# Three of the seven weight combinations of the last stage are split into two halves when they are made, and stored and loaded as halves

## The chip, the cores and the metric

The kernel runs on one core of one Trainium2 chip. The metric is the device time of one execution in microseconds. The engines are TensorE (PE), VectorE (DVE), ScalarE (ACT), GpSimd (POOL) and SyncE (SP), which here issues the DMA transfers. Line numbers are those of the kernel before.

## The reference

```python
A = sm(q, k_lm); Bm = sm(q_lm, k_lm); C = sm(q_lm, k)      # softmax of scaled products, 32 landmarks
Z = ...                                                    # start of the iteration
for _ in range(6):
    Z = 2 * Z - Z @ Bm @ Z
x = A @ Z @ C @ v                                          # 4 x 8 heads, 576 tokens, head size 64
x = x.reshape(2304, 512)
h = x @ w_in                                               # first FFN, d_ff 2048
x = np.maximum(0.01 * h, h) @ w_out
xn = x / np.sqrt(np.mean(x * x, axis=-1, keepdims=True) + 1e-06) * rms_g
g = xn @ w_gate                                            # second FFN, d_ff 1536
out = (g / (1 + np.exp(-g)) * (xn @ w_val)) @ w_out2
```

All inputs and the output are fp32.

## The kernel before

**Precision.** Large products run as three passes on fp32r halves: an operand x is split into hi (x cast to fp32r) and lo (x minus hi, in fp32r), and a product is the sum of three terms of halves. So each operand of a large product costs a cast on ACT or DVE and a subtraction on DVE or POOL (`split_steps`, L1330) before PE can use it.

**Stages.** Until some 391 us the landmark attention runs beside the first FFN: `chain` (L598) makes the scores and the iteration with many small fp32 matmuls (b<-qt,kt, b<-kt,qsum, b<-rz, b<-ident,e), and between these stand the units of the first FFN, six matmuls b<-at,mm (L1140) and twelve py<-gs,w (L1211) each. From there to 657 us the first half of the second FFN runs (`gv`, L1619): the products with w_gate and w_val as 36 groups, each of which is a block of tokens b and a block f of columns. The order of the groups is (f, b) = (0,0), (1,0), (0,1), (1,1), (0,2), (1,2) and so on. From 657 us `out_pair` (L1875) runs nine pairs of the product with w_out2.

**Seven products.** Both halves of the second FFN use seven products in place of eight, on combinations of the operands' quarters: for the right-hand operand these are B11, B21, B22, T1, T2, T3 and T4. A group does them in this order, each six matmuls in three passes: A11 B11, S2 T2, S3 T3, S1 T1, A12 B21, A22 T4, S4 B22. `gv_rest` (L1661) adds them up on DVE: `gs<-hs,b` when the second is there, `gs<-gs,py` twice (for the third and the fourth), `ct<-gs,py` (c21, for the sixth) and `ct<-gs,py` (c12, for the last), with the products `us<-hs,ct` and `us<-ct,gs` behind them. Each addition also gives a bank of PSUM back to PE.

**Operands of gv.** `prep_x(b)` (L1529) makes the combinations of x of one block of tokens: the subtractions for T1, T3, T2 and T4 go to POOL or DVE, in the tiles called `misc`, and each is split into tiles called at, mm or w. The first group that needs block b is number 2b. `prep_w` does the same for the gate and value weights, from the `raw` tiles that w_gate, w_val, w_out2 are loaded to.

**Operands of the last stage.** `prep_o(p)` (L1717) makes, for six pairs of blocks of w_out2 rows, the seven combinations in the two `raw` tiles of the pair, and stores each (128 KB) in DRAM (`store_o`, L1735, 42 stores, 155 to 250 us). `load_o(k)` (L1749) loads each combination for the last stage, 768 KB, when its place is free, from 624 to 661 us; then `split_o` (L1762) splits it in two halves with a cast and a subtraction of 768 columns each. `prep_u` (L1819) prepares the left-hand operand u from DRAM.

**Order.** No order is written out. A planner (class `Order`, L93) takes steps (`yield`) of many tasks, each with a due time, costs and its possible engines (`pool_dve` is POOL or DVE, `act(n) + dve2(n)` ACT or DVE), and always places the step that is best by its own table of costs. Each engine runs its instructions in the placed order, SP its DMA issues too. So a change of a few steps can move every later instruction.

Of the kernel before, what the change touches and what calls it, by code (L numbers as in the profile page):

```python
# [9 lines left out]
F32 = mybir.dt.float32  # L10
F32R = mybir.dt.float32r
# [8 lines left out]
P = 128  # L20
# [207 lines left out]
def pe(n, count=1, more=0):  # L228
    return [("pe", int(count * (n * 0.4258 + 10.3)) + more)]
# [10 lines left out]
def act(n):  # L240
    return [("act", n + 50)]
# [6 lines left out]
def dvep(n):  # L248
    return [("dvep", int(n * 1.04) + 67)]


def dve2(n):
    return [("dvep", int(n * 0.52) + 68)]


def pool(n):
    return [("pool", int(n * 2.1) + 150)]


def pool_dve(n):  # L260
    return pool(n) + dvep(n)


def sp(nbytes):
    return [("sp", int(nbytes / 360))]


def pause(ns=0):
    return [(None, ns)]


def landing(ns, now):
    return [(None, ns + 2500 * (now > 30000))]
# [3 lines left out]
def landmark_attention_then_two_ffns(  # L277
# [13 lines left out]
    nc = tc.nc  # L291
# [22 lines left out]
    dram = ctx.enter_context(tc.tile_pool(name="dram", bufs=1, space=DRAM))  # L314
# [9 lines left out]
    order = Order(PAR["window"], PAR["slope"], PAR["bias"], rings)  # L324
# [24 lines left out]

    HM = DM // 2  # L350
    NP2 = NF2 // 2
    wo_dram = [dram.tile([P, NP2, HM], F32, name=f"wo_dram{k}") for k in range(7)]
    u_dram = dram.tile([P, NF2, NT], F32, name="u_dram")

# [55 lines left out]
    def after(made):  # L410
# [9 lines left out]
    nc = SimpleNamespace(  # L420
        scalar=nc.scalar, vector=order.vector, gpsimd=Seen(nc.gpsimd, after), tensor=nc.tensor,
        sync=nc.sync,
    )
    engine = {"act": nc.scalar, "dve": nc.vector, "pool": nc.gpsimd}

    def copy(e, out, src):
        if e == "act":
            nc.scalar.copy(out, src)  # L428
        else:
            engine[e].tensor_copy(out, src)  # L430
# [828 lines left out]
    B11, B21, B22, T1, T2, T3, T4 = range(7)  # L1259
# [70 lines left out]
    def split_steps(parts):  # L1330

        for hi, lo, src, n in parts:
            e = yield act(n) + dve2(n), []
            copy(e, hi, src)
            e = yield pool(n) + dvep(n), []
            engine[e].tensor_sub(lo, src, hi.bitcast(F32))
# [380 lines left out]
    def prep_o(p):  # L1717

        yield pause(0), [f"out2 {2 * p}", f"out2 {2 * p + 1}"]
        (ra, ta), (rb, tb) = o_raw[2 * p], o_raw[2 * p + 1]  # L1720
        a, b = (t.bitcast(F32).rearrange("p (k n) -> p k n", n=HM) for t in (ta, tb))
        src = {B11: a[:, 0], T1: a[:, 2], T2: a[:, 3],
               B21: b[:, 0], B22: b[:, 1], T3: b[:, 2], T4: b[:, 3]}
        sums = {T1: (a[:, 1], a[:, 0]), T3: (b[:, 1], a[:, 1]),
                T2: (b[:, 1], a[:, 2]), T4: (b[:, 0], a[:, 3])}
        for k in (B11, B21, B22):
            order.aside(store_o(p, k, src[k]))
        for k in (T1, T3, T2, T4):
            e = yield pool_dve(HM), []
            engine[e].tensor_sub(src[k], *sums[k])  # L1730
            order.aside(store_o(p, k, src[k]))
        yield pause(0), [f"o{p},{k}" for k in range(7)]
        order.free(ra, rb)

    def store_o(p, k, t):  # L1735
        yield sp(P * 1024), []
        nc.sync.dma_start(wo_dram[k][:, p], t)
        yield pause(2500), []
        order.done(f"o{p},{k}")

    ND = NP2 * P
    o_home = {}
# [5 lines left out]

    def load_o(k):  # L1749
        at, off, event = o_place[k]  # L1750
        yield sp(P * 4 * NP2 * HM), [event] + [f"o{p},{k}" for p in range(NP2)]
        v = home[at][:, off:off + OW].rearrange("p (t a n) -> p t a n", t=2, n=HM)
        o_home[k] = v
        hi, lo = v[:, 0], v[:, 1]
        nc.sync.dma_start(lo.bitcast(F32), wo_dram[k])
        yield landing(3000, order.now), []
        order.done(f"o_in{k}")
        order.add(
            due_o(0) + o_order.index(k) * PAR["pair"] // 7, PAR["split_o"], split_o(k, hi, lo)
        )  # L1760

    def split_o(k, hi, lo):  # L1762
        yield pause(0), [f"o_in{k}"]
        h = NP2 // 2
        yield from split_steps([
            (hi[:, x:x + h], lo[:, x:x + h], lo[:, x:x + h].bitcast(F32), h * HM) for x in (0, h)
        ])
        order.done(f"wo{k}", early=600)
# [106 lines left out]
    def out_pair(n):  # L1875
        pp, t = {}, {}

        def step(name, l, r, tag=None, needs=()):
            yield pe(HM, 3 * NP2), list(needs) + ([(tag, 1)] if tag else []) + [
                f"U{n},{l}", f"wo{r}"  # L1880
            ]
            if tag:
                pp[name] = bank(tag)
            hi, lo = u_hl[n, l]
            m = 0
            for x, i in ((hi, 0), (hi, 1), (lo, 0)):
                for p in range(NP2):
                    nc.tensor.matmul(  # L1888
                        pp[name][:, :HM], x[:, p, :], o_home[r][:, i, p, :],
                        start=(tag is not None and m == 0), stop=(m == 3 * NP2 - 1),  # L1890
                        skip_group_check=True,
                    )
                    m += 1
            order.free(hi)
# [70 lines left out]
    with tc.manual_schedule():  # L1965
# [28 lines left out]
        def due_o(n):  # L1994

            return due2(len(seq)) + PAR["pair"] * n
# [27 lines left out]
        for p in range(NP2):  # L2024
            order.add(due(PAR["o_from"] + PAR["o_step"] * (2 * p + 2)), 0, prep_o(p))


        for b in range(B):
            when = first(lambda j, f: j == 2 * b)
            for g in range(NG):  # L2030
                before = PAR["chain"][b] + PAR["load"] - g * 200 + PAR["form"]
# [23 lines left out]
        def start_second():  # L2055
            yield pause(0), [f"a{NB - 1},{g}" for g in range(NG)] + [
                f"chain{B - 1},{g}" for g in range(NG)
            ]
            att.release()
            open_p2a()  # L2060
            nc.sync.dma_start(g_sb, rms_g)
            nc.scalar.mul(g_sb, g_sb, 0.375 * DM ** 0.5 * 2.0 ** -24)
            order.done("p2a")
            for j in range(NB):
                order.add(due2(j // 2), PAR["norm"], norm(j))
            for b in range(NGR):
                for h in range(2):
                    order.add(due2(place[0, b]), PAR["prep"], load_x(b, h))
                order.add(due2(place[0, b]), PAR["prep"], prep_x(b))
            for f in range(NF2):  # L2070
                order.add(due2(place[f, 0]), PAR["prep"], prep_w(f))
            order.add(due2(0), 0, gv(0))
            for i, k in enumerate(o_order):
                order.add(due_o(0) + i * PAR["pair"] // 7, PAR["load_o"], load_o(k))
            for n in range(NG2):
                order.add(due_o(n), PAR["load_u"][min(n, 2)], load_u(n))
                order.add(due_o(n), PAR["prep_u"], prep_u(n))
            order.add(due_o(0), 0, out_pair(0))
# [66 lines left out]
```

## Time and profile before

| | us |
|---|---|
| median of 3 runs (796.16 to 796.9) | 796.31 |
| the profiled execution | 798.18 |
| its span, first to last instruction | 796.4 |
| PE busy | 786.6 |
| DVE busy | 597.0 |
| ACT busy | 345.0 |
| POOL busy | 145.1 |

The granted clock of TensorE is 1.00 of full speed throughout. A timeline row gives the start, the recorded duration, the engine and line, the operation and its tiles (out<-in, the names of the program), the shape, how many of the same stand in the row, and in brackets how long the engine had been idle ahead of it and for what. Operations that DVE runs back to back overlap in the records, so that the distance from start to start is shorter than the duration.

### The profile page before, as it was taken

Reading aid. Unit: us, or ns where it says so; the run is one execution under the profiler, and the core shown is the slowest. Engines: PE = TensorE matmul, PEld = TensorE weight load, DVE = VectorE, ACT = ScalarE, POOL = GpSimd, SP = SyncE. Lnnn points to the kernel's source line nnn. Section 1 sums busy time; section 2 is a strip of 40 time slices with the busy share of each in tenths; the row PEclk is TensorE's granted clock in tenths of the full one; section 3 lists DMA queues with packets and bytes.
Section 4 is the critical chain, followed back from the end, with each engine's and each line's share of the span. In section 5 each row is a group of like instructions: output and inputs, shape, how many; then the busy total and the mean of one; then the engine's idle time right before and its main releaser. Section 6 shows DMA issues by size and latency. Waiting matters only on the chain. (4 is left out here: it accounts for less than half of the span.)

```text
span 796.4 us, 16707 instructions
## 1 busy us (share of the span) xinstructions
PE 786.6 (99%) x6508; PEld 748.7 (94%) x6508; DVE 597.0 (75%) x1202; ACT 345.0 (43%) x777; POOL 145.1 (18%) x183
## 2 busy tenths in 40 slices
PE   8999999999999999999999999999999999999998
PEld 7687996999999879999999999999999999999998
DVE  5997867844556776579998777676666699999981
ACT  4885365433434548655752332223232164332220
POOL 2535100000013332111222421122221000000000
PEclk9999999999999999999999999999999999999999
DMA  9985645565446134455411432322331595555501
GB/s 326 356 303 144 206 151 148 170 196 187 159 138 211 58 117 157 156 175 147 129 42 59 166 113 93 109 69 90 112 112 56 165 332 170 146 146 158 161 27 54
DMA packets 84320, 119.72 MB, mean 150 GB/s; under 512 B 7824, under 2 KB 62608, under 8 KB 84240
## 3 DMA queue, kind: packets, MB, share of 16 engines
q1 hardware_dynamic: 84240, 118.64, 45.4%
q8 instruction: 51, 0.84, 0.4%
q14 instruction: 29, 0.24, 0.1%
HBM read 81.86 MB, written 36.77 MB: 149 GB/s over the span
## 5 line engine op out<-in xcount | busy, mean ns | idle before, releaser
L1211 PE MATMUL py<-gs,w 128*128 128x288 f32 x1536 | 223.2, 296 | 1.2 <-issue 0.9
L1211 PEld LDWEIGHTS py<-gs,w 128*128 128x128 f32 x1536 | 208.8, 188 | 10.0 <-issue 7.3
L1140 PE MATMUL b<-at,mm 128*128 128x288 f32 x768 | 120.3, 297 | 0.8 <-DVE mm L74 0.7
L1140 PEld LDWEIGHTS b<-at,mm 128*128 128x128 f32 x768 | 106.9, 188 | 7.1 <-issue 4.0
L1158 ACT ACTIVATE gs<-b 128x288 fp32r<-128x288 f32 x128 | 52.5, 410 | 112.9 <-PE b L1140 94.4
L74 DVE TENSOR_TENSOR gs<-hs,gs 128x288 fp32r<-128x288 f32 x95 | 45.8, 486 | 52.0 <-ACT hs L1161 44.1
L74 DVE TENSOR_TENSOR ct<-gs,py 128x384 f32<-128x384 f32 x72 | 39.5, 549 | 27.8 <-PE py L1613 27.8
L74 POOL TENSOR_TENSOR gs<-hs,gs 128x288 fp32r<-128x288 f32 x33 | 27.0, 817 | 156.4 <-ACT hs L1161 120.3
L1683 ACT ACTIVATE hs<-b 128x384 f32<-128x384 f32 x36 | 17.7, 492 | 86.6 <-PE b L1613 86.6
L74 DVE TENSOR_TENSOR gs<-gs,py 128x384 f32<-128x384 f32 x72 | 39.7, 552 | 16.7 <-PE py L1613 14.4
L1161 ACT ACTIVATE hs<-b 128x288 f32<-128x288 f32 x128 | 52.3, 408 | 0.0
L1712 ACT ACTIVATE ct<-ct 128x384 f32<-128x384 f32 x36 | 18.9, 526 | 69.4 <-DVE ct L74 69.4
L1613 PE MATMUL b<-w,wt 128*128 128x384 f32 x180 | 35.4, 337 | 0.0
L1613 PE MATMUL b<-w,mm 128*128 128x384 f32 x180 | 35.4, 337 | 0.0
L1613 PE MATMUL py<-w,wt 128*128 128x384 f32 x180 | 34.6, 338 | 0.1
L1613 PE MATMUL py<-w,mm 128*128 128x384 f32 x180 | 34.6, 336 | 0.0
L474 ACT ACTIVATE raw<-raw 128x512 f32<-128x512 f32 x52 | 33.8, 677 | 0.0
L1613 PEld LDWEIGHTS py<-w,mm 128*128 128x128 f32 x180 | 31.6, 188 | 0.4 <-DVE gs L74 0.3
L1613 PEld LDWEIGHTS py<-w,wt 128*128 128x128 f32 x180 | 31.7, 188 | 0.3 <-DVE gs L74 0.3
L1613 PEld LDWEIGHTS b<-w,wt 128*128 128x128 f32 x180 | 31.9, 188 | 0.0
L1613 PEld LDWEIGHTS b<-w,mm 128*128 128x128 f32 x180 | 31.8, 188 | 0.0
L74 DVE TENSOR_TENSOR gs<-hs,b 128x384 f32<-128x384 f32 (+1 forms) x45 | 23.5, 523 | 9.5 <-PE b L1613 4.9
(309 smaller groups left out, 1534.4 us busy)
## 6 DMA issues: line engine op xcount, KB each, us to landing
u_dram<-us SPq DMA_DIRECT2D x36, 384.0 KB, 2.3
raw<-w_out SPq DMA_DIRECT2D x20, 512.0 KB, 4.4
y_dram<-ys SPq DMA_DIRECT2D x56, 144.0 KB, 1.9
yin<-u_dram SPq DMA_DIRECT2D x20, 384.0 KB, 5.1
raw<-w_gate SPq DMA_DIRECT2D x12, 512.0 KB, 4.1
raw<-w_val SPq DMA_DIRECT2D x12, 512.0 KB, 5.0
wo_dram<-raw SPq DMA_DIRECT2D x42, 128.0 KB, 1.8
qt<-qT SPq DMA_DIRECT2D x8, 576.0 KB, 6.7
```

The costliest lines, as they stand in the source:

```text
L74: self.last = make(*args, **kwargs)
L474: nc.scalar.activation(high.bitcast(F32), high.bitcast(F32), AF.Prelu, scale=2.0 ** -112, alpha=2.0 ** 32)
L1140: nc.tensor.matmul(ph[:, :SB], w[b, c][:, g, o:o + P], x[j][:, g, :], start=(n == 0), stop=(n == 3 * NG - 1),)
L1158: nc.scalar.activation(g_hi[u], ph[:, :SB], AF.Prelu, alpha=0.01)
L1161: nc.scalar.activation(hs, ph[:, :SB], AF.Prelu, alpha=0.01)
L1211: nc.tensor.matmul(yacc[i][d][:, :SB], w[f][:, d * P:(d + 1) * P], x[u], start=(f == f0 and n == 0), stop=(f == f1 - 1 and n == 2),)
L1613: nc.tensor.matmul(pp[:, :GB], w[f][:, i, c * P:(c + 1) * P], x[b][k][:, c, :], start=(first and n == 0), stop=(n == 5), skip_group_check= ...
L1683: nc.scalar.activation(sg, pp["a"][:, :GB], AF.Silu)
L1712: nc.scalar.activation(t["c12"], t["c12"], AF.Silu)
```

## The change

For T4, B22 and B21 (`apart`) the split is done when the combination is made: `apart_o` casts it into a quarter of the `raw` tiles that is spare by then (or becomes spare when B11 or T1 of the pair is stored), subtracts in place, and stores both halves, 128 KB each, in `wo_parts`. `load_o` loads both halves at once, 1536 KB, straight to their places, and there is no `split_o` for these three. The other four combinations stay as they were.

```diff
+    wo_parts = [dram.tile([P, 2, NP2, HM], F32, name=f"wo_parts{k}") for k in range(7)]
...
+        spare_at = {T4: (a[:, 1], []), B22: (a[:, 0], [f"o{p},{B11}"]),
+                    B21: (a[:, 2], [f"o{p},{T1}"])}
         for k in (B11, B21, B22):
-            order.aside(store_o(p, k, src[k]))
+            if k not in apart:
+                order.aside(store_o(p, k, src[k]))
...
+        for k in apart:
+            order.aside(apart_o(p, k, src[k], *spare_at[k]))
...
+    apart = (T4, B22, B21)
+
+    def apart_o(p, k, t, hi, before):
+        yield pause(0), before
+        hi = hi.bitcast(F32R)
+        yield from split_steps([(hi, t.bitcast(F32R), t, HM)])
+        for i, part in enumerate((hi.bitcast(F32), t)):
+            yield sp(P * 1024), []
+            nc.sync.dma_start(wo_parts[k][:, i, p], part)
+        yield pause(2500), []
+        order.done(f"o{p},{k}")
...
+        if k in apart:
+            nc.sync.dma_start(v.bitcast(F32), wo_parts[k])
+            yield landing(3000, order.now), []
+            order.done(f"wo{k}")
+            return
         nc.sync.dma_start(lo.bitcast(F32), wo_dram[k])
```

Since the planner places everything anew, instructions move on every engine from some 155 us on. Three places follow; w_1582 and w_1589 are the same tile, as are w_113 and w_120, and lines of the new program are one to 26 higher.

DVE, from the last additions of group (0,1)'s successor (1,1) to the first of group (0,2), before; the cast mm<-misc and the subtraction mm<-misc,mm of 128x768 under it are T2 of block 2, whose sum POOL has made:

```order
L74 TENSOR_TENSOR mm<-misc,mm 128x768
L74 TENSOR_TENSOR gs_5339<-gs_5339,py 128x384 x2
L74 CAST mm<-misc 128x768
L74 TENSOR_TENSOR misc<-yin,misc 128x768
L74 TENSOR_TENSOR ct<-gs_5339,py 128x384
L74 TENSOR_TENSOR mm<-misc,mm 128x768
L74 TENSOR_TENSOR us<-hs,ct 128x384
L74 TENSOR_TENSOR ct<-gs_5339,py 128x384
L74 TENSOR_TENSOR at<-misc,at 128x768
L74 TENSOR_TENSOR us<-ct,gs_5339 128x384
L74 TENSOR_TENSOR gs_5339<-hs,b_5639 128x384
```

And now:

```order
L74 TENSOR_TENSOR ct<-gs_5385,py 128x384
L74 TENSOR_TENSOR mm<-misc,mm 128x768
L74 TENSOR_TENSOR us<-hs,ct 128x384
L74 TENSOR_TENSOR ct<-gs_5385,py 128x384
L74 TENSOR_TENSOR misc<-q,misc 128x2x96
L74 TENSOR_TENSOR misc<-ys,misc 128x2x288
L74 TENSOR_TENSOR us<-ct,gs_5385 128x384
L74 CAST mm<-misc 128x768
L74 TENSOR_TENSOR misc<-yin,misc 128x768
L74 TENSOR_TENSOR mm<-misc,mm 128x768
L74 TENSOR_TENSOR at<-misc,at 128x768
L74 TENSOR_TENSOR gs_5385<-hs,b_5696 128x384
```

The two rows that make the sum of T2 (misc<-q,misc and misc<-ys,misc) came from POOL to DVE, and the whole of T2 went from ahead of both ct additions to behind them.

PE in the last chain, at some 259 to 270 us, before; L948 and L631 are the small fp32 groups, L1140 and L1211 the first FFN:

```order
L1211 MATMUL py<-gs,w_1582 128x288 x12
L948 MATMUL b_3632<-qt,kt 32x288 x4
L948 MATMUL b_3633<-qt,kt 32x288 x4
L631 MATMUL b_3648<-kt,qsum_3587 32x304 x4
L631 MATMUL b_3653<-kt,qsum_3627 32x304 x4
L1140 MATMUL b_3666<-at,mm 128x288 x6
L631 MATMUL b_3676<-kt,qsum_3587 32x304 x4
L631 MATMUL b_3681<-kt,qsum_3627 32x304 x4
L1211 MATMUL py<-gs,w_113 128x288 x12
```

And now:

```order
L1212 MATMUL py<-gs,w_1589 128x288 x12
L949 MATMUL b_3660<-qt,kt 32x288 x4
L949 MATMUL b_3661<-qt,kt 32x288 x4
L1141 MATMUL b_3674<-at,mm 128x288 x6
L632 MATMUL b_3690<-kt,qsum_3614 32x304 x4
L632 MATMUL b_3695<-kt,qsum_3654 32x304 x4
L1212 MATMUL py<-gs,w_120 128x288 x12
L632 MATMUL b_3732<-kt,qsum_3614 32x304 x4
L632 MATMUL b_3737<-kt,qsum_3654 32x304 x4
L1141 MATMUL b_3752<-at,mm 128x288 x6
```

Where two fp32 groups stood with one first-FFN group between them, there are three with two between them; a little further on, another such group stands apart.

SP, the loads ahead of the last stage, before (w, wt and mm take B21, T4 and B22; the u loads are those of the second block):

```order
L1755 DMA w_1582<-wo_dram_80 128x1536
L1700 DMA u_dram<-us 128x768
L1810 DMA w_1582<-u_dram 128x6x128 x2
L1810 DMA at<-u_dram 128x6x128 x2
L1755 DMA wt<-wo_dram_85 128x1536
L1755 DMA mm<-wo_dram_81 128x1536
L1700 DMA u_dram<-us 128x768 x2
L1810 DMA yin<-u_dram 128x6x128 x4
```

And now:

```order
L1777 DMA w_1589<-wo_parts_80 128x3072
L1701 DMA u_dram<-us 128x768
L1777 DMA wt<-wo_parts_85 128x3072
L1777 DMA mm<-wo_parts_81 128x3072
L1701 DMA u_dram<-us 128x768
L1836 DMA w_1589<-u_dram 128x6x128 x2
L1836 DMA at<-u_dram 128x6x128 x2
L1701 DMA u_dram<-us 128x768
L1836 DMA yin<-u_dram 128x6x128 x4
```

The four u loads stood ahead of T4 and B22 and stand now behind both, which are twice as long, and behind a store.

## Rows read from the trace of the kernel before

**Rows 1.** The page's busy times (share, instructions), and PE's waits: us, times, longest.
```profile
PE 786.6 (99%) x6508; PEld 748.7 (94%) x6508; DVE 597.0 (75%) x1202; ACT 345.0 (43%) x777; POOL 145.1 (18%) x183
...
PE b L1888 <- ACT q L428: 0.6, 1, 0.6
PE b L1443 <- DVE ct L74: 0.4, 1, 0.4
```

**Rows 2.** Windows: stretch, length, busy us of each engine, clock, DMA share, GB/s.
```profile
160.00:225.00 65.00, 65.00 (x516) 62.43 (x515) 32.90 (x74) 25.35 (x64) 4.60 (x6) 1.00 0.56 181
...
440.00:660.00 220.00, 220.00 (x1266) 220.00 (x1265) 158.94 (x294) 69.17 (x134) 45.69 (x54) 1.00 0.39 132
660.00:675.00 15.00, 14.85 (x126) 14.65 (x124) 15.00 (x22) 6.69 (x11) 0.00 (x0) 1.00 0.55 163
```

**Rows 3.** Timeline of DVE from the first group of block 1 to block 2.
```profile
397.82 1.76 DVE L74 TENSOR_TENSOR w<-misc,w 128x768 fp32r<-128x768 f32 x1
...
409.52 0.55 DVE L74 TENSOR_TENSOR gs<-hs,b 128x384 f32<-128x384 f32 x1 [0.50 <-PE b L1613]
410.59 0.55 DVE L74 TENSOR_TENSOR gs<-gs,py 128x384 f32<-128x384 f32 x1 [0.51 <-PE py L1613]
...
413.26 0.35 DVE L74 TENSOR_TENSOR at<-q,at 128x192 fp32r<-128x192 f32 x1
...
414.20 0.55 DVE L74 TENSOR_TENSOR ct<-gs,py 128x384 f32<-128x384 f32 x1
...
418.44 1.21 DVE L74 TENSOR_TENSOR gs<-gs,py 128x384 f32<-128x384 f32 x2
420.70 1.08 DVE L74 CAST mm<-misc 128x768 fp32r<-128x768 f32 x1 [1.05 <-POOL misc L74]
...
423.03 0.94 DVE L74 TENSOR_TENSOR mm<-misc,mm 128x768 fp32r<-128x768 f32 x1
423.90 0.55 DVE L74 TENSOR_TENSOR us<-hs,ct 128x384 f32<-128x384 f32 x1
424.37 0.54 DVE L74 TENSOR_TENSOR ct<-gs,py 128x384 f32<-128x384 f32 x1
```

**Rows 4.** Timeline of DVE, a cast of the same size in the first FFN.
```profile
371.74 0.56 DVE L74 CAST w<-misc 128x768 fp32r<-128x768 f32 x1
```

**Rows 5.** Timeline of POOL beside the cast at 420.70.
```profile
420.61 0.75 POOL L74 TENSOR_TENSOR misc<-misc 128x256 f32<-128x256 f32 x1
```

**Rows 6.** Timeline of PE, products of the third, fourth and fifth group.
```profile
409.33 1.22 PE L1613 MATMUL py<-w,wt 128*128 128x384 f32 x6
...
421.92 1.20 PE L1613 MATMUL b<-w,wt 128*128 128x384 f32 x6
422.96 0.86 PE L1613 MATMUL b<-mm,wt 128*128 128x384 f32 x4
424.03 0.62 PE L1613 MATMUL b<-mm,wt 128*128 128x384 f32 x2 [0.22 <-DVE mm L74]
```

**Rows 7.** Timeline of PE in the last chain: a plain group, one between fp32 groups.
```profile
248.71 0.95 PE L1140 MATMUL b<-at,mm 128*128 128x288 f32 x6
...
262.08 1.06 PE L1140 MATMUL b<-at,mm 128*128 128x288 f32 x6
```

**Rows 8.** Timeline of PE and DVE at the start of the last stage.
```profile
672.58 2.27 PE L1888 MATMUL b<-q,mm 128*128 128x256 f32 x18
673.20 0.41 DVE L74 TENSOR_TENSOR us<-gs,py 128x256 f32<-128x256 f32 x1
...
675.45 2.41 PE L1888 MATMUL b<-q 128*128 128x256 f32 x18 [0.60 <-ACT q L428]
```

**Rows 9.** DMA issues on SP (timeline), and windows as in rows 2.
```profile
645.44 1.45 SPq L1810 DMA_DIRECT2D w<-u_dram  x2
...
644.00:658.00 14.00, 14.00 (x83) 14.00 (x82) 13.53 (x22) 10.11 (x16) 1.84 (x1) 1.00 1.00 316
658.00:668.00 10.00, 10.00 (x86) 10.00 (x86) 10.00 (x15) 4.51 (x8) 0.00 (x0) 1.00 0.40 132
```

More of the change, by code (lines that the diff above doesn't have):

```diff
@@ L1730, in prep_o @@
             engine[e].tensor_sub(src[k], *sums[k])
-            order.aside(store_o(p, k, src[k]))
+            if k not in apart:
+                order.aside(store_o(p, k, src[k]))
+        for k in apart:
+            order.aside(apart_o(p, k, src[k], *spare_at[k]))
         yield pause(0), [f"o{p},{k}" for k in range(7)]
         order.free(ra, rb)
+    apart = (T4, B22, B21)
[8 more added lines that the diff above has]
+        order.done(f"o{p},{k}")
     def store_o(p, k, t):
@@ L1750, in load_o @@
         at, off, event = o_place[k]
-        yield sp(P * 4 * NP2 * HM), [event] + [f"o{p},{k}" for p in range(NP2)]
+        yield sp(P * 4 * NP2 * HM * (1 + (k in apart))), [event] + [
+            f"o{p},{k}" for p in range(NP2)
+        ]
         v = home[at][:, off:off + OW].rearrange("p (t a n) -> p t a n", t=2, n=HM)
```

## The prediction

> **What bounds the kernel now.** I looked first at the waits of TensorE, because PE is busy 786.6 us of the span [rows 1]: a kernel like this gains or loses only where PE stops or does more. Its waits come to a few microseconds, and two of them lie at places that the change touches, 0.6 us for a cast at the start of the last stage and 0.4 us for a DVE result in a norm [rows 1]. Then the windows: in the stretch where the weights of the last stage are made, PE is busy 65.00 of 65 us and DVE 32.90; from 440 to 660 us PE has no gap at all; at the start of the last stage DVE is busy 15.00 of 15 us and PE loses only 0.15 [rows 2]. Last come the timelines of DVE, POOL and PE around one hand-over of the second FFN [rows 3 to 6], found from the order of the changed program: it is the one place where the new order puts a long chain of one engine straight in front of PE.
>
> All durations are of the profiled execution, 798.18 us with a span of 796.4; the median of the runs is 796.31. A change in the span is added to the median, since the 1.8 us around the span stay. A measurement of this kernel can tell some 0.2% (1.6 us) from no change.
>
> **Part 1: splitting early, and storing halves.** 18 casts and 18 subtractions of 128x256 are added at some 155 to 285 us, spread over ACT, DVE and POOL, and 18 more stores of 128 KB. PE is full in that stretch and DVE half idle [rows 2], and nothing there feeds PE within microseconds, so I take nothing for them; without that cover 18 pairs would cost some 18 x 0.6 us (a third of the 0.87 us of a 128x768 pass each [rows 3]), 11 us. What they do cost is order: the planner re-places everything behind them. In the last attention chain the small fp32 groups (qt,kt and kt,qsum) no longer stand in a row, so PE changes between fp32 and fp32r twice more, in and out. An h group of six between two such groups is recorded with 1.06 us, a plain one with 0.95 [rows 7]. Four changes at 0.11 us are +0.4 us; bounds 0 and 0.9.
>
> **Part 2: the hand-over to the third token block, where the time goes.** Before, POOL made T2 of this block (misc<-q,misc and misc<-ys,misc), and DVE only cast it: the cast began at 420.70, having waited 1.05 us for POOL, and PE reached its second product at 422.96 and the third pass of it at 424.03, 0.22 us late [rows 3, 6]. In the new order POOL has other work, and DVE makes T2 itself, *behind* the c12 addition (ct<-gs,py) of the group before. That addition needs the last product of that group, which ends when the next group starts, at 421.92. So a chain on one engine now lies between the end of one group and the second product of the next:
> PE's end is seen by DVE some 0.19 us later (409.33 against 409.52 [rows 3, 6]): 422.11. c12 takes 0.47 us (like the one from 423.90), the two pieces of T2 0.94 (like the two from 413.26 to 414.20), us<-ct,gs 0.47, all start to start: 423.99 [rows 3]. The cast of 128x768 is 0.56 recorded where DVE has SBUF to itself, which is 0.48 start to start [rows 4]; beside a POOL operation it was 1.08 [rows 3, 5]. With 0.48 the high half is there at 424.47, and PE has stood since 422.96: 1.5 us. Two of the three passes of the product take 2/3 of 1.04 us and end at 425.2. The low half needs the T4 subtraction (0.87) and its own 0.87, with 0.08 to its recorded end: 426.3. The third pass starts there instead of at 424.03: +2.25 us if DVE comes to c12 on time.
>
> Does it? Ahead of c12, DVE now has three more passes of 128x768 (3 x 0.87), two more casts (2 x 0.48), the two pieces of T3 (0.94) and one copy less (0.5): +4.0 us. Its cover: before, DVE was through with the same list at 419.65 (418.44 and 1.21), the two operations still to come before c12 take 0.93, so there are 1.5 us to 422.11, and two idle gaps of 0.50 and 0.51 [rows 3]. That leaves it 1.5 us late. Against it, DVE passes that ran beside POOL took 1.76 us and not 0.95 (397.82 [rows 3]); with the POOL work gone one such pass returns 0.8 us. I take 0.8 us late. Together +3.0 us; bounds 2.2 (on time) and 4.3 (1.5 late, the cast at 1.08). PE is busy without gaps behind this place [rows 2], so nothing gives it back.
>
> On this sum a rule bears that the trace does not carry. The sum above takes start to start; DVE's record from 423.90 has 0.55 us and the next starts at 424.37, inside it [rows 3]. The Trainium skill (VectorE: DVE Perf Modes, The DRAIN you can't avoid) says that the next operation does not start before the pipe of the one ahead is empty. If that meant the recorded end, each of the eight links would be 0.08 us longer and the term 3.6 us; the rows speak for start to start.
>
> **Part 3: the start of the last stage.** Six subtractions of 0.87 us leave DVE and six casts leave ACT; two casts come to DVE instead. The PE wait there is 0.60 us at 675.45, for the cast q<-misc of S2 of the second token block [rows 1, 8]. That chain begins with us<-gs,py, which needs the end of the product ahead of 672.58 and ran only at 673.20, behind a 0.87 us pass. With DVE free it can run at 672.7, and the chain moves 0.5 us forward, leaving 0.1. So the 5.2 us of DVE work are worth -0.5 us (bounds -0.6 and 0): the other subtractions were already hidden. The tail of the kernel is untouched.
> The loads of the three combinations are doubled to 1536 KB. The u loads of the second block, issued from 645.44 before, now stand behind T4, B22 and a store, so at some 654.5 to 657 us. DMA is full to 658 (316 GB/s) and drops to 132 GB/s in the ten microseconds behind it [rows 9]. What is left to move after 658 is then those 1.32 MB and 2.36 MB more, 3.68 MB, which take 11.6 us at 316 GB/s: all is landed by 669.6, the four u loads ahead of the last store and load, at some 665 to 668. DVE wants the first at about 670 to 672. It fits, by 2 to 5 us: nothing.
>
> **Part 4, small.** The 0.4 us wait of the norm [rows 1] is for a DVE operation beside which POOL ran; the new order moves POOL's work, so -0.2, the middle between losing the wait and keeping it.
>
> Sum: +0.4 + 3.0 - 0.5 - 0.2 = +2.7 us: a span of 799.1, a profiled execution of 800.9, and 796.31 + 2.7 = 799.0 us.
>
> **Rivals.**
> A, not slower: the T2 chain is hidden. DVE runs c12 and T2 well before PE asks, as it did with POOL's help (PE waited 0.22 us). For it: DVE has idle time before this place and loses POOL's interference. Against it: c12 cannot begin before 421.92 whatever DVE does, since it reads the last product, and program order on DVE is fixed. It decides if PE's second product came more than 2.2 us later than 422.96 for another reason. Then -0.5 - 0.2 + 0.4 = -0.3: 796.0.
> B, the waits go and the new order costs nothing anywhere: -0.6 - 0.4 = -1.0: 795.3, still within what can't be told from no change.
> C, DMA: the doubled T4 and B22 loads push the u loads past the point where DVE wants them; each microsecond later than 671 is a microsecond of PE. For it: the loads stand ahead of them in the queue, and the stretch is full. Against it: the slack above. If the 3.68 MB go at the mean of the two windows, 224 GB/s, they take 16.4 us and the last lands at 674.4: +3 on top of the sum, about 802.
> D, DVE is the bound through the first five groups: neither its idle gaps nor POOL's absence cover anything. It is then late by 4.0 - 1.5 = 2.5 us: 0.4 + 2.25 + 2.5 - 0.7 = +4.5, about 800.8.
>
> **How the numbers follow.** Forecast 0.62 (799.0, own range 797.7 to 800.4), A 0.16, B 0.06, C 0.08, D 0.08. The range holds A down to 796.0 and reaches to 801.0 on the other side, leaving out most of B and C and half of D: 0.18. Slower by over 0.2% (797.9 and above): most of the forecast, C and D, 0.74. Within: A, B and the low end of the forecast, 0.22. Faster (below 794.7): only if B is larger than any wait that I can see, 0.04.
>
> **What would show it.** In the trace of after: a wait of PE at the second product of the fifth group (b<-mm,wt), 1.2 to 2.5 us on the DVE cast and about 1 us on the subtraction, and none of over 0.3 us there proves part 2 wrong. The wait at the cast q<-misc in the last stage falls to 0.1 to 0.2 us; if it stays, part 3 is wrong. Two more changes of form in the last chain, without waits. The u loads of the second block land before 670; a PE or DVE wait on a DMA behind 667 us speaks for C. Long waits of PE on c22 at 398 to 420 us speak for D. A time below 796 says that the order mattered less than I think.

## The result and the profile after

The changed kernel takes 801.84 us (median of 4 runs, 800.72 to 802.53) against 796.27 us; the ratio taken run against run is 1.0059, with a 95% interval of 1.0045 to 1.0073. That is +4.7 us (3.6 to 5.8), where +2.7 was forecast; the two medians alone lie 5.6 us apart, within that interval. The profiled execution, 800.72 us with a span of 798.9, is the shortest of the four.

PE's waits in the trace after (us in total, times, longest), the three that answer to [rows 1] and to the 0.22 us in [rows 6]:

```profile
PE b L1614 <- DVE mm L74: 2.6, 2, 2.4
...
PE py L1614 <- DVE gs L74: 0.6, 1, 0.6
...
PE b L1914 <- ACT q L429: 0.2, 1, 0.2
```

The largest wait is new and stands at the second product of the fifth group. The timeline of PE there, of after (answers to [rows 6]):

```profile
403.68 2.38 PE L1614 MATMUL py<-w,mm 128*128 128x384 f32 x12 [0.55 <-DVE gs L74]
...
420.59 1.21 PE L1614 MATMUL b<-w,wt 128*128 128x384 f32 x6
424.22 1.55 PE L1614 MATMUL b<-mm,wt 128*128 128x384 f32 x4 [2.43 <-DVE mm L74]
425.96 1.01 PE L1614 MATMUL b<-mm,wt 128*128 128x384 f32 x2 [0.19 <-DVE mm L74]
426.76 2.73 PE L1614 MATMUL py<-mm,wt 128*128 128x384 f32 x12
```

And DVE's, answering to [rows 3]; the last row but one is the cast that PE waits for:

```profile
420.41 0.95 DVE L74 TENSOR_TENSOR mm<-misc,mm 128x768 fp32r<-128x768 f32 x1
421.28 0.55 DVE L74 TENSOR_TENSOR us<-hs,ct 128x384 f32<-128x384 f32 x1
421.75 0.55 DVE L74 TENSOR_TENSOR ct<-gs,py 128x384 f32<-128x384 f32 x1
422.21 0.35 DVE L74 TENSOR_TENSOR misc<-q,misc 128x192 f32<-128x192 f32 x1
422.48 0.75 DVE L74 TENSOR_TENSOR misc<-ys,misc 128x576 f32<-128x576 f32 x1
...
423.62 0.55 DVE L74 CAST mm<-misc 128x768 fp32r<-128x768 f32 x1
...
424.95 0.95 DVE L74 TENSOR_TENSOR mm<-misc,mm 128x768 fp32r<-128x768 f32 x1
```

Group four ends and group five begins on PE at 420.59. c12 (ct<-gs,py) could start 0.2 us later, at 420.8, and starts at 421.75: DVE is 1.0 us late. From there row follows row without idle time to the cast's end at 424.17 (423.62 and 0.55), and PE goes on at 424.22. What was not in the forecast is in the durations of the matmuls behind the wait: 1.55 us for four and 2.73 for twelve, where [rows 6] has 0.86 for four and the other rows of twelve 2.28. The windows of after show why (columns as in rows 2; the third number from the end is the granted clock):

```profile
420.00:424.00 4.00, 1.79 (x11) 1.47 (x9) 4.00 (x9) 1.00 (x2) 0.00 (x0) 1.00 0.02 4
424.00:426.00 2.00, 1.59 (x5) 1.08 (x5) 1.97 (x4) 0.83 (x1) 0.00 (x0) 0.59 0.51 197
426.00:428.00 2.00, 2.00 (x7) 2.00 (x8) 1.45 (x2) 0.00 (x0) 0.00 (x0) 0.56 0.00 0
428.00:430.00 2.00, 2.00 (x13) 2.00 (x12) 1.52 (x3) 0.00 (x0) 0.00 (x0) 1.00 0.02 4
```

After the wait PE gets 0.59 and 0.56 of full speed, so it runs at the lower of its two levels, 1.2 GHz, for most of these 4 us. The Trainium skill (TensorE: Matmul & The Clock Gate, Part 1) says that the throttled state is the default, and that activity releases it. The trace agrees as far as it goes: the clock fell behind 2.43 us in which PE stood. In the kernel before, no wait behind PE's first matmul is longer than 0.95 us, and the clock stays at 1.00 behind it; the 1.4 us for which L1044 waits there lie ahead of PE's first matmul and say nothing on this.

The last group of matmuls starts 2.35 us later in after (793.31 against 790.96). Where these lie, from the starts of the same product in before and after:

| place | before | after | difference | step |
|---|---|---|---|---|
| first FFN, ahead of the change | 135.40 | 134.25 | -1.15 | not the change: both orders are the same up to here |
| first FFN, behind the last chain | 294.64 | 293.46 | -1.18 | -0.03, early work and changes of form |
| second FFN, first product | 390.95 | 389.23 | -1.72 | -0.54, the norm's wait is gone |
| fifth group, first product | 421.92 | 420.59 | -1.33 | +0.39, c22 late in group two |
| fifth group, third pass of T2 | 424.03 | 425.96 | +1.93 | +3.26, the T2 chain |
| fifth group, product with T4 | 427.65 | 430.39 | +2.74 | +0.81, lower clock |
| last stage, S2 of block 2 | 675.45 | 677.80 | +2.35 | -0.39, last stage |

The steps behind the first row make +3.5 us. The -1.15 us in the first row come mostly from PE's first 25 matmuls, 6.31 us in before and 4.98 in after: at first one takes some 0.24 us from start to start, later 0.13, and the time of the turn differs from trace to trace (the 25 take 4.97 us in warm, 5.47 in ap_T4). The clock column reads 1.00 there all the same, so "throughout", said of the clock of before, is not shown for the first 7 us.

The other three runs of the changed kernel are 1.0 to 1.8 us longer than the profiled one, at a mean granted clock of 0.995 to 0.996 against 0.998. On a span of 800 us that is an estimated 1.6 to 2.4 us more of lacking full-speed time, so these runs lost more to the lower clock; no trace shows where.

The start of the last stage, of after (answers to [rows 8]), and DMA windows of the same stretch as in [rows 9]:

```profile
675.53 0.42 DVE L74 TENSOR_TENSOR us<-gs,py 128x256 f32<-128x256 f32 x1
...
677.80 2.42 PE L1914 MATMUL b<-q 128*128 128x256 f32 x18 [0.20 <-ACT q L429]
```

```profile
644.00:658.00 14.00, 14.00 (x82) 14.00 (x81) 13.20 (x22) 7.83 (x13) 1.84 (x1) 1.00 0.92 341
658.00:668.00 10.00, 10.00 (x80) 10.00 (x79) 10.00 (x16) 3.51 (x6) 0.00 (x0) 1.00 1.05 340
```

us<-gs,py now runs 0.2 us behind the end of its product (675.33) and the chain behind it costs 0.20 and not 0.60 us. DMA is full to 668 us, 340 GB/s where [rows 9] has 132, and neither PE nor DVE waits for it. The four u loads (w and at) land from 666.9 to 670.9 us, by the trace's landings.

### The profile page after: what moved, and what is told of

Same layout as the page of the kernel before. It is cut to its first block, busy times and chain, and to the rows that moved or that the text cites. A ratio compares the mean times of both kernels' runs of the same rounds, so it can differ in the third digit from the quotient of the medians.

```text
span 798.9 us, 16762 instructions
## 1 busy us (share of the span) xinstructions
PE 786.9 (99%) x6508; PEld 748.6 (94%) x6508; DVE 604.0 (76%) x1228; ACT 341.6 (43%) x777; POOL 142.3 (18%) x181
## 5 line engine op out<-in xcount | busy, mean ns | idle before, releaser
L74 POOL TENSOR_TENSOR misc<-misc 128x256 f32<-128x256 f32 (+1 forms) x30 | 25.4, 850 | 58.5 <-DVE misc L74 30.6
L429 ACT COPY hs<-b 128x384 f32<-128x384 f32 (+1 forms) x42 | 18.7, 444 | 31.0 <-PE b L1914 24.5
```

The lines of the kernel that those rows point to most:

```text
L74: self.last = make(*args, **kwargs)
```

## The experiments

Two names: **the order** is where the planner puts the instructions, **the work** are the casts, subtractions, stores and longer loads that the change adds.

**1. The same work, without the order (quiet).** In the kernel before, the splits are put in behind the seven steps of a pair without steps of their own, so that the planner's order does not change until the loads of the last stage.

```diff
         yield pause(0), [f"o{p},{k}" for k in range(7)]
+        for k, x in ((T4, a[:, 1]), (B22, a[:, 0]), (B21, a[:, 2])):
+            hi = x.bitcast(F32R)
+            copy("act", hi, src[k])
+            nc.vector.tensor_sub(src[k].bitcast(F32R), src[k], hi.bitcast(F32))
+            nc.sync.dma_start(wo_parts[k][:, 0, p], hi.bitcast(F32))
+            nc.sync.dma_start(wo_parts[k][:, 1, p], src[k])
         order.free(ra, rb)
```

> The change with the order of before: the planner's steps stay those of the kernel before until the loads of the last stage; the 18 casts (ACT), 18 subtractions (DVE) and 36 half stores are put in behind the seven steps of each pair without a step of their own. Everything is computed. If the new order alone makes the loss (theory O), the fifth group starts its second product without the 2.43 us wait, the granted clock stays 1.00 and only the gain at the start of the last stage is left: 795.9 us, 0.3 to 0.6 below before. If the early work or the doubled loads cost by themselves (theory W), the time stays above before, 798 to 801 us, with waits at 155 to 290 us or behind 655 us.

Measured: 1.0009 (1.0000 to 1.0018), 797.16 us, between the times of the two theories. The wait and the lower clock of the fifth group are gone, so the order makes the large loss, as theory O has it; but the gain did not come out, since the work is not free after all. Timelines of SP, DVE and PE of this run (two places of the first FFN, then the last stage):

```profile
213.81 0.81 SPq L457 DMA_DIRECT2D raw<-w_out  x2
...
217.73 0.43 DVE L74 TENSOR_SCALAR raw<-raw 128x512 uint32<-128x512 uint32 x1 [2.25 <-DMA raw<-w_out]
...
223.00 2.26 PE L1212 MATMUL py<-gs,w 128*128 128x288 f32 x15 [0.69 <-DVE ys L74]
...
674.29 2.32 PE L1904 MATMUL b<-q 128*128 128x256 f32 x18
```

The raw tiles are held longer, so the next load of w_out is issued at 213.8 us where before had 207.3; DVE, which works in order, waits 2.25 us for it, and PE stands behind DVE's ys sums. Against before, PE loses 1.4 us around this place. In the last stage the wait at the cast q<-misc is gone altogether: 0.86 us, more than the 0.6 us of the wait itself.

**2. One combination, with either order (ap_T4, ap_B21).** The changed kernel with one combination in the list, which is the same work both times.

```diff
-    apart = (T4, B22, B21)
+    apart = (T4,)
```

In ap_B21 the line reads `apart = (B21,)`.

> Only T4 is split early, planned as in the changed kernel; the rows of DVE and POOL from 385 to 430 us then stand as in before. Theory O: no wait at the second product of the fifth group, 796.0 to 796.5 us, the same as before (two of six subtractions leave the last stage). Theory W: a third of the loss, some 797.5 to 798 us.

> Only B21 is split early: the same amount of work as with T4 alone, but the rows of DVE and POOL at the hand-over stand as in the changed kernel (c12, then T2 on DVE). Theory O: the whole loss, wait of some 2.4 us and a lower granted clock behind it, 800.5 to 802.5 us. Theory W: a third of the loss, 797.5 to 798 us.

Measured: ap_T4 1.0004 (0.9995 to 1.0013), ap_B21 1.0055 (1.0038 to 1.0072). One third of the work makes the whole loss or none of it, by the order that it happens to bring (B22 alone was not run). The cast of T2 in ap_T4 (first row, DVE) waits for POOL as in [rows 3]; the second product in ap_B21 (second row, PE) waits for DVE as in the changed kernel, and the clock behind it falls to 0.50:

```profile
419.84 1.09 DVE L74 CAST mm<-misc 128x768 fp32r<-128x768 f32 x1 [1.05 <-POOL misc L74]
```

```profile
424.12 2.75 PE L1614 MATMUL b<-mm,wt 128*128 128x384 f32 x6 [2.42 <-DVE mm L74]
```

**3. What a wait of PE costs beyond its length (stall).** In the kernel before, an addition that PE's next bank depends on is repeated in seven groups, far from the change.

```diff
         nc.vector.tensor_add(f32("c22", "c22"), t["u2"], pp["c"][:, :GB])
+        for _ in range({8: 2, 11: 3, 14: 4, 17: 5, 20: 6, 23: 7, 26: 8}.get(i, 0)):
+            nc.vector.tensor_add(t["c22"], t["u2"], pp["c"][:, :GB])
```

> Before, with the addition of the third product (gs<-gs,py) repeated 2, 3, 4, 5, 6, 7 and 8 times in groups 8, 11, 14, 17, 20, 23 and 26, so that PE waits for its bank some 0, 0.6, 1.3, 1.8, 2.5, 3.0 and 3.8 us there. Nothing is left out. The question is what a wait costs beyond its length. Theory K (a lone stop of PE lowers the granted clock): behind the longer waits matmuls of 384 columns take up to twice their time for some microseconds and the granted clock falls below 1.00, behind the short ones not; a wait of 2.5 us costs about 1 us more than its length. Theory N (the low clock in the changed kernel comes from something else there): the clock stays 1.00 throughout and the time rises by the sum of the waits alone, some 13 us: 809 us.

Measured: 813.19 us. Timeline of PE, the waits, and two windows, ahead of and behind the wait of 2.07 us:

```profile
477.81 2.35 PE L1613 MATMUL py<-at,mm 128*128 128x384 f32 x12 [0.31 <-DVE gs L74]
501.01 2.38 PE L1613 MATMUL py<-at,wt 128*128 128x384 f32 x12 [0.89 <-DVE gs L74]
524.84 2.35 PE L1613 MATMUL py<-at,mm 128*128 128x384 f32 x12 [1.49 <-DVE gs L74]
549.22 3.91 PE L1613 MATMUL py<-at,wt 128*128 128x384 f32 x12 [2.07 <-DVE gs L74]
575.65 3.33 PE L1613 MATMUL py<-at,mm 128*128 128x384 f32 x12 [2.67 <-DVE gs L74]
602.79 3.18 PE L1613 MATMUL py<-at,wt 128*128 128x384 f32 x12 [3.25 <-DVE gs L74]
```

```profile
546.00:549.00 3.00, 1.15 (x7) 0.83 (x5) 2.83 (x6) 1.00 (x2) 0.00 (x0) 1.00 0.00 0
549.00:551.00 2.00, 1.78 (x6) 1.78 (x7) 0.72 (x2) 0.00 (x0) 0.00 (x0) 0.61 0.00 0
551.00:553.00 2.00, 2.00 (x9) 2.00 (x8) 1.11 (x2) 0.00 (x0) 0.00 (x0) 0.54 0.00 0
```

Behind waits of 0.31 to 1.49 us twelve matmuls take 2.35 to 2.38 us, as ever; behind 2.07 us and more they take 3.2 to 3.9 us, at a clock of 0.61 and 0.54 behind the first of these three. Theory K holds: the waits sum up to 10.7 us, and this one execution is some 16.6 us over the median of before (15.0 by the spans of the two profiles). That leaves 4 to 6 us for three stretches of lower clock.

**4. Keeping PE at work during the wait (warm).** The changed kernel with 12 matmuls on operands that are ready, ahead of the product that waits.

```diff
+            if i == 4 and name == "b":
+                for _ in range(6):
+                    for c in range(KD // 2):
+                        nc.tensor.matmul(
+                            pp[name][:, :GB], w_hi[f][:, l, c * P:(c + 1) * P], x_hi[b][B11][:, c, :],
+                            start=True, stop=True, skip_group_check=True,
+                        )
             product(pp[name], f, b, l, r, tag is not None)
```

> The changed kernel with 12 matmuls of 384 columns more, put ahead of the second product of the fifth group; they use operands that are ready and write the bank which the product then starts anew, so nothing of the result changes. They fill 2.1 of the 2.43 us that PE waits there, and DVE's chain does not depend on them. If the lower granted clock behind the wait is a part of the loss (theory K), the wait falls to some 0.4 us, the clock stays 1.00 and the products behind it take their usual time: 1 to 2.5 us less than the changed kernel (its runs lay at 800.7 to 802.5), 799.0 to 800 us, ratio to before 1.003 to 1.0045. If the low clock does not matter (theory N), the time stays at 801 to 802 us, ratio 1.006.

Measured: 1.0033 (1.0020 to 1.0045). Timeline of PE and a window of this run:

```profile
420.82 2.24 PE L1636 MATMUL b<-w,wt 128*128 128x384 f32 x12
423.41 0.97 PE L1614 MATMUL b<-mm,wt 128*128 128x384 f32 x4 [0.35 <-DVE mm L74]
425.15 0.62 PE L1614 MATMUL b<-mm,wt 128*128 128x384 f32 x2 [0.77 <-DVE mm L74]
425.61 2.28 PE L1614 MATMUL py<-mm,wt 128*128 128x384 f32 x12
```

```profile
424.00:426.00 2.00, 1.23 (x8) 0.90 (x7) 1.97 (x3) 0.83 (x1) 0.00 (x0) 1.00 0.36 141
```

The cast comes no earlier, the clock stays at 1.00, and the loss shrinks from 1.0059 to 1.0033: by the ratios the lower clock costs 2.1 us (0.26% of 796) on top of the wait, with some 1.5 us either way for the two intervals. In the two profiled executions the product with T4 comes 0.8 us nearer to the start of its group. What is left, +2.6 us, is the wait and the small steps of the table. The third pass now waits 0.77 us, which the slow passes in the changed kernel had covered.

**5. Who makes T2, and when (t2pool, t2first, t2early).** Three versions of the changed kernel that touch T2 of the third block alone. t2pool gives the sum to POOL:

```diff
-            e = yield pool_dve(n), [f"T1 {b}"]
+            e = yield pool(n) if b == NGR - 1 else pool_dve(n), [f"T1 {b}"]
             y1_sub(e, tb, d1, ta, True)
```

> The changed kernel with only the sum of T2 of block 2 on POOL, as before; four rows of DVE change and the cast goes to ACT. If it matters who makes T2 (theory P), the wait at the second product of the fifth group falls to below 0.5 us, as before the change. If it matters when the tile of T3 is free (theory L: the sum of T2 overwrites it, and the subtraction that reads it ends only at 421.3 us), POOL starts at 421.3, takes 2.0 us, the cast 0.8: PE starts its second product at 424.2, as in the changed kernel, wait 2.4 us.

Measured: 801.23 us. Timelines of POOL and PE:

```profile
421.67 0.59 POOL L74 TENSOR_TENSOR misc<-q,misc 128x192 f32<-128x192 f32 x1 [12.47 <-DVE us L74]
422.22 1.40 POOL L74 TENSOR_TENSOR misc<-ys,misc 128x576 f32<-128x576 f32 x1
```

```profile
424.54 0.96 PE L1614 MATMUL b<-mm,wt 128*128 128x384 f32 x4 [2.98 <-ACT mm L429]
```

PE waits 2.98 us, at least as long as before this edit. The subtraction of T3 that reads the tile ends at 421.12 in this trace; POOL starts at 421.67, released by the DVE row behind it. So giving the sum to POOL does not help: what counts is when DVE is through with T3 (one execution).

t2first and t2early put T2's sum, cast and low half in right behind the low half of T3, t2first on DVE, t2early with T3's low half, T2's sum and its low half on POOL and the cast on ACT:

```diff
+                if b == NGR - 1 and k == T3:
+                    y1_sub("dve", tb, d1, ta, True)
+                    copy("dve", x_hi[b][T2], tb)
+                    engine["dve"].tensor_sub(x_lo[b][T2], tb, x_hi[b][T2].bitcast(F32))
```

In t2early the three engines are "pool", "act" and "pool". The later steps of T2 of this block are left empty in both.

> The changed kernel with T2 of block 2 (sum, cast, low half) still on DVE, but ahead of us<-hs,ct and c12 instead of behind. If the wait comes only from c12 standing ahead of T2 (theory C), the wait of 2.4 us falls to some 1.0 us and nothing follows: 798.5 us. If DVE as a whole is too late at this place (theory L), the first wait falls to 1.0 us but the third addition comes later and PE waits some 1.8 us there: the sum of the waits stays near 3 us; with no wait over 2 us the granted clock should stay 1.00, and the time is some 1 us below the changed kernel, 800 us.

Measured: 1.0051 (1.0030 to 1.0071). Timeline of PE and windows:

```profile
422.62 1.61 PE L1628 MATMUL b<-mm,wt 128*128 128x384 f32 x6 [1.27 <-DVE mm L74]
...
429.63 2.35 PE L1628 MATMUL py<-at,wt 128*128 128x384 f32 x12 [2.25 <-DVE gs L74]
```

```profile
428.00:430.00 2.00, 0.37 (x2) 0.40 (x3) 1.90 (x4) 0.00 (x0) 0.00 (x0) 1.00 0.01 4
430.00:434.00 4.00, 4.00 (x25) 3.99 (x24) 3.91 (x9) 1.52 (x3) 0.73 (x1) 1.00 0.66 202
```

Theory L: DVE as a whole is late. The first wait halves, and the next addition is late by 2.25 us. The time cannot be told from that of the changed kernel (1.0059). So T2's place behind c12 is not the whole cause: moved ahead, it hands its delay on to the next addition. The clock stays at 1.00 here even behind 2.25 us; why it fell behind 2.07 us in stall and not here stays open.

> The changed kernel with one step of block 2 moved: the low half of T3, the sum of T2, its cast (ACT) and its low half are put in right behind the cast of T3, on POOL, which stands idle there from 409 to 430 us; DVE loses these rows, every other row keeps its place. Theory O (the place of T2 in the order makes the loss): no wait at the second product of the fifth group, at most 0.3 us at the product with T4 behind it, granted clock 1.00; some 4 us less than the changed kernel, 796 to 797 us. Rival W (early work and doubled loads cost by themselves): 799 us or more in spite of it.

Measured: 1.0072 (1.0058 to 1.0085), the highest ratio of all. That is in the range of rival W, but not for its reason. Timelines of DVE, POOL and PE, and a window:

```profile
413.84 2.43 DVE L74 TENSOR_TENSOR w<-yin,w 128x768 fp32r<-128x768 f32 x1
...
417.53 1.71 DVE L74 TENSOR_TENSOR w<-yin,w 128x768 fp32r<-128x768 f32 x1
...
419.63 1.78 DVE L74 TENSOR_TENSOR at<-q,at 128x192 fp32r<-128x192 f32 x1
```

```profile
413.59 1.86 POOL L74 TENSOR_TENSOR mm<-misc,mm 128x768 fp32r<-128x768 f32 x1 [4.86 <-ACT mm L429]
...
416.69 1.73 POOL L74 TENSOR_TENSOR misc<-ys,misc 128x576 f32<-128x576 f32 x1
419.36 1.83 POOL L74 TENSOR_TENSOR mm<-misc,mm 128x768 fp32r<-128x768 f32 x1 [0.94 <-ACT mm L429]
```

```profile
419.76 1.33 PE L1628 MATMUL py<-w,mm 128*128 128x384 f32 x6 [1.82 <-DVE gs L74]
422.60 1.98 PE L1628 MATMUL py<-w,mm 128*128 128x384 f32 x6 [1.51 <-DVE gs L74]
```

```profile
424.00:426.00 2.00, 2.00 (x8) 2.00 (x8) 1.08 (x2) 0.00 (x0) 0.00 (x0) 0.50 0.00 0
```

The wait at T2 is gone, as meant, but POOL at work draws out DVE's rows beside it, 2.43 us for one that takes 0.95 and 1.78 for one that takes 0.35, and PE waits 1.82 and 1.51 us for the additions ahead. The Trainium skill (GPSIMD Engine Reference, Key points) says that GpSimd shares its SBUF interfaces with VectorE and contends with its instructions of two SBUF inputs; the trace agrees, and shows the price, 3.3 us of PE in these two waits.

DVE's rows here are held rather than slowed: the three end 0.82, 0.82 and 0.22 us behind the end of POOL's row beside them (415.45, 418.42, 421.19), each 0.13 us less than it takes alone, as if it began only when POOL was about done. In before it is the same: the cast at 420.70 ends 0.42 us behind POOL's row at 420.61 [rows 3, 5] and takes 0.56 alone [rows 4]. And behind the two waits, neither as long as 2 us, the clock falls too, to 0.50, where the expectation had 1.00. So this run does not decide between O and W.

**6. The work without the order, made cheaper (quiet2, quiet3, quiet3b).** quiet2 is quiet with the subtractions on POOL.

> The change with the order of before, as in the run named quiet, but with the 18 early subtractions on POOL in place of DVE. There PE lost 1.4 us at 223 us, 0.69 of it a wait for DVE's ys sum, and got back 0.5 us at a norm at 380 us and 0.86 us at the start of the last stage. If DVE's early work made that loss, it is gone: 0.9 to 1.4 us below before, some 795.5 us. If the casts on ACT or the stores made it, the time stays within 0.2 us of quiet, 0.7 us above before.

Measured: 1.0020 (1.0011 to 1.0029), so slower than before and not faster; the load is issued at 213.7 us and PE waits 0.69 us at 222.9 as in quiet. The engine of the subtractions did not make that loss. In the profiles quiet2 is 0.65 us longer than quiet, and about that lies at the norm, where PE waits 0.56 us and in quiet not at all.

quiet3 puts the three splits in where T4 was stored, so that the raw tiles come free earlier; quiet3b does the same with casts on ACT and subtractions on POOL.

```diff
     def store_o(p, k, t, pair=None):
         yield sp(P * 1024), []
-        nc.sync.dma_start(wo_dram[k][:, p], t)
+        if k not in apart:
+            nc.sync.dma_start(wo_dram[k][:, p], t)
+        if k == T4:
+            a, src = pair
...
```

What follows there are the lines of quiet for T4, B22 and B21.

> The change with the order of before again, but the three splits of a pair (cast and subtraction on DVE) and their six stores are put in where T4 was stored, not behind all seven steps. In quiet and quiet2 the raw tiles were held so long that the next load of w_out was issued at 213.8 us and not at 207.3, DVE waited 2.2 us for it at 217.6 and PE 0.69 us behind DVE. If that hold made the loss of 1.4 us (theory H), the load is issued by some 210 us, neither DVE nor PE waits at 217 to 223 us, and the 0.86 us at the start of the last stage are left as a gain: some 795.7 us, 0.1% below before. If the early work on the engines made it, the loss stays and the time is 0.5 us or more above before.

> As quiet3, with the early casts on ACT and the early subtractions on POOL. In quiet3 the load of w_out was in time, but PE lost 0.65 us at 160 us behind DVE, which had six of the early operations ahead of its ys sums. If that is DVE's work (theory D), the loss at 160 us is gone and the 0.86 us at the start of the last stage are left: 0.1% below before, some 795.7 us. If POOL beside DVE costs as much (theory B), DVE's operations are drawn out there and the time stays within 0.05% of before.

Measured: quiet3 0.9999 (0.9990 to 1.0009), quiet3b 0.9996 (0.9987 to 1.0004). The load is issued at 208.2 us in quiet3 (212.2 in quiet3b) and neither DVE nor PE waits for it: the hold of the tiles was the cause (theory H). In quiet3, PE lost 0.65 us at 160 us to three waits of 0.15 to 0.18 for DVE's ys sums; in quiet3b nothing changes against before from 136 us to the last stage, where the 0.86 us are gained (theory D in the trace). A gain of that size is 0.1%, and no version could be told from before by its runs.

## Why the prediction was right, and where its size was off

- **Place and direction.** Part 2 named the second product of the fifth group, and the mechanism: T2 behind c12 on DVE. The step there is +3.26 us at the third pass where +3.0 was forecast, DVE 1.0 us late where 0.8 was taken (1.5 less the 0.8 that POOL's absence returns is 0.7), the wait for the cast 2.43 us where 2.3 follows from both. The sum from start to start held: from 421.75 to the cast's end at 424.17 are 2.42 us where it gave 2.36; the recorded durations added up make 2.75. That is what the rule which the prediction cites (the Trainium skill, VectorE: DVE Perf Modes, The DRAIN you can't avoid: the next operation does not start until the pipe is empty) would have given if it meant the recorded end; the rows speak for start to start. ap_B21, ap_T4 and quiet show that this order is enough for the loss, and that without it this loss is gone. The third pass waited 0.19 and not 1.1 us only because the two passes ahead of it ran at the lower clock. What the prediction had as a side question, whether DVE comes to c12 on time, is the deeper half of the mechanism: t2first took T2 out from behind c12, and the loss stayed, as a wait for the next addition.
- **The size.** What failed is the list of costs: it ends with the wait, and has no term for the granted clock behind it. Measured, that term is 0.8 us in the profiled execution and 2.1 us over the runs (warm). With it the sum of +2.7 becomes +4.8, and +4.7 was measured; warm, without it, lies at +2.6. That both agree to 0.1 us is in part luck. Each ratio is known to about 1 us only; and without the clock the steps of the table do add up to +2.7, but because misses cancel: parts 1 and 4 came out 0.4 and 0.3 us lower than forecast, part 2, part 3 and the wait on c22, which was not in the sum, 0.3, 0.1 and 0.4 us higher. From the 796.31 us of before, +4.7 is 801.0 us: above the forecast's own range of 797.7 to 800.4, and at the upper end of the wide one; the plain median, 801.84, lies beyond that. As a number D's 800.8 is nearer, but D has DVE 2.5 us late and not 1.0. The rows of before gave no sign of this term: behind PE's first matmul they have no wait over 0.95 us, all at a clock of 1.00. But part 2 itself forecast a stop longer than any of these, and so outside of what the rows cover; a rival should have said so.
- **Part 1.** Over the early work PE's starts moved by 0.03 us only, in the planner's order, so the zero was right there, and the +0.4 us for changes of form were not: h groups at the changed places are recorded with 1.06 us as in [rows 7], but the starts behind the chain moved by nothing. The trace shows why: from the h group at 248.71 to the one at 294.64 (in after 247.55 to 293.46) the fp32r matmuls take 0.2 us more from start to start, 35.83 for 35.62, so the changes cost half of what was taken, and the fp32 ones take 0.2 us less, 10.08 for 10.31. A part of that is that an fp32 group apart takes 0.64 us (259.55 to 260.19) and two in a row took 1.37 (260.71 to 262.08). The cover was worth less than I wrote: with the same work put in blindly PE lost 0.65 to 1.4 us, not by lack of time on DVE but because a raw tile came free later and because DVE's sums stood behind it.
- **Part 3.** -0.39 us where -0.5 was forecast, for the reason given; a wait of 0.20 us stays. That the other subtractions were hidden is right. The loads came in time for PE and DVE, so rival C did not happen, but the slack was less than reckoned: the four u loads landed from 666.9 to 670.9 us and not at 665 to 668, the last behind the 670 that stood as a sign.
- **Part 4.** The norm's wait went wholly, -0.54 for -0.2. It is between 0 and 0.6 us in runs whose order there is that of before, so it says little.
- **Rivals.** A and B would have needed the order of before. D, a DVE bound through five groups, shows in one wait of 0.55 us on c22 of group two, and in t2first, where a gain at T2 came back as a wait behind it: DVE had no time to spare there, so D was partly right, with DVE 1.0 us late and not 2.5.

## What to carry to other kernels

Where a planner or scheduler places the work, a small edit is judged by the order that it brings, not by its own cost: one of three equal edits cost 0.55% here and another nothing (the third was not run alone). Read the new order for the place where the engine that sets the time comes to wait for a chain on another engine that starts with its own last result; sum that chain start to start, and add what the slower clock behind a long stop costs. Where the engine ahead is short of time as a whole, moving one step of it forward only moves the wait. Moving a step to an idle POOL is not free while DVE is busy beside it.

## What the runs showed of the hardware that I had not expected

- The granted clock fell to 0.50 to 0.56 in the lowest window of 2 us behind stops of TensorE of 2.07, 2.67 and 3.25 us (stall), 2.43 us (after), 2.42 us (ap_B21) and 2.98 us (t2pool), and behind two stops of 1.82 and 1.51 us with six matmuls between them (t2early); matmuls of 384 columns took nearly twice their time there. It stayed at 1.00 behind 1.49 us (stall) and once behind 2.25 us (t2first). So the length of a stop does not decide alone, and these runs do not show what does.
- A 128x192 subtraction on DVE took 1.78 us and not 0.35 while POOL worked on a 128x768 one, and ended 0.22 us behind POOL's row: it stood until POOL was about done (t2early).
